# When next bits, totals and last values are issued in a hashed attention with a ReLU-squared feed-forward

## The chip, the cores and the metric

The kernel runs on one core of a Trainium2 chip. The metric is the device time of one launch in microseconds (us). In the profile the engines are PE (TensorE's matrix products) and PEld (its weight loads), DVE (VectorE), ACT (ScalarE), POOL (GpSimd) and SP (SyncE, which here only issues transfers). A line such as L419 is line 419 of the kernel before. A name with a q, such as POOLq, is the engine's sequencer.

## The reference, cut to what matters

```python
# q, k, v: (4, 8, 768, 64); proj: (64, 6); w_in: (512, 2048); w_out: (2048, 512)
q_bits = (einsum('bhsd,dk->bhsk', q, proj) > 0)
k_bits = (einsum('bhsd,dk->bhsk', k, proj) > 0)
mask = bucket(q_bits)[..., :, None] == bucket(k_bits)[..., None, :]   # all 6 bits agree
scores = where(mask, q @ k.T / sqrt(64), -1e9)
attn = softmax(scores)                       # rows divided by their sum + 1e-9
x = (attn @ v) as (3072 tokens, 512)         # heads side by side
h = x @ w_in
out = (max(h, 0) ** 2) @ w_out
```

Two queries and keys see each other only if their six hash bits agree. What comes out of the attention goes through a feed-forward layer with a squared ReLU.

## The kernel before, in words

The program is written in the order in which each engine shall issue (a manual schedule): engines run beside each other, each takes its own instructions in order, and waits between them follow from the data.

**Pairs.** The 32 heads are worked on as 16 pairs (`pr` from 0 to 15, `NP` is 16). In a pair the two heads lie in the two halves of the 128 partitions. Keys are cut into 6 blocks of 128 (`kt`), queries into two halves of 384 (`i`). `score(pr, kt, i)` makes one block of scores in PSUM: products of the bits (which push pairs of unequal bits far down) and products of the features, and then one ACT operation, exp, writes the result to `e`, a ring of four tiles (L459). Twelve such scores make a pair.

**Values.** `attend(pr, kt, s)` adds the products of `e` with the values to the accumulator `xo`, 64 rows of the array by 64 columns at a time; s says which half of the rows goes with which half of the queries. A pair's products lag behind its scores, so `attend(old, 4, 0)`, `attend(old, 5, 0)`, `attend(old, 4, 1)` and `attend(old, 5, 1)` of the pair before stand between the first scores of a pair. Whenever s changes, `part` (lines 499 to 504) puts a step between the last product before and the first product after: an empty instruction on POOL (L502) that waits for the one, and that the other waits for. In an even pair this comes at `attend(old, 4, 1)`, `attend(pr, 0, 1)` and `attend(pr, 2, 0)`; in an odd pair also in the sums of the totals.

**Totals.** `add_up` (L490, L495, DVE) adds the `e` of the six key blocks. In an odd pair, `sums_and_hashes` sums the totals of the two pairs before over the partitions by products with ones (`tot`, L564), and between them hashes the next two pairs (L382) and takes the signs (L401, ACT). `invert` (L600 to L608, DVE) makes the reciprocals, `spread` (L618, ACT) lays them out, `normalize` (L624, L630, DVE) multiplies the values kept by `keep_x` (L538, ACT), and one transfer on SP's queue writes them to `x_all` in DRAM.

**Bits of the next pair.** After the signs, `weigh` (L408, ACT) scales them, and `place_bits` (L419) sends eight transfers on POOL's queue that put them where the next pair's scores read them. There are two buffers of bits, for even and odd pairs. Before, both come in the middle of each pair: the weighing after `score(pr, 2, 1)`, the transfers after `attend(pr, 0, 1)`.

**Weights beside.** Between these steps each pair also rounds one piece of the 64-bit weights (`part_power`, `place_power`, `part_top`, `round_weight`), and from pair 4 on `sum_in` makes sums of weight blocks that the feed-forward part needs; 16 of them are dealt out over the pairs.

**After the attention.** The feed-forward part takes tokens in 3 chunks of 1024 and saves products by sums of blocks (a scheme of seven products for eight). `sum_x(0, n)` makes the four differences of x blocks for the first chunk, on DVE; `product` (L899) runs the seven products, with x and a unit of weights (`w_unit`) in the first two and a difference in the third. The first chunk's x was loaded during pairs 9 to 12. `keep_busy` at the very start makes products whose result nobody uses, while the first inputs are on their way.

Of the kernel before, what the change touches and what calls it, by code (L numbers as in the profile page):

```python
# [34 lines left out]
def kernel(  # L35
# [315 lines left out]
    busy = const.tile([P, P], BF16, name="busy")  # L351
    void = ps_o.tile([P, 2, 512], FP32, name="xo")

    def keep_busy(n):

        wide = busy.rearrange("p (o n) -> p o n", o=1).to_broadcast([P, 4, P])
        for _ in range(n):
            nc.tensor.matmul(
                out=void[:, 0].rearrange("p (o n) -> p o n", o=4), lhsT=busy, rhs=wide,
                start=True, stop=True,  # L360
            )

# [122 lines left out]
    def add_up(pr, kt):  # L485

        e = key_of(pr, kt)[:, :, :, 0:HS]
        if kt == 1:
            totals[pr] = to_add[(pr + 1) % 2]
            nc.vector.scalar_tensor_tensor(  # L490
                out=totals[pr], in0=key_of(pr, 0)[:, :, :, 0:HS], scalar=SB * TINY,
                in1=e, op0=ALU.add, op1=ALU.add,
            )
        else:
            nc.vector.tensor_tensor(out=totals[pr], in0=totals[pr], in1=e, op=ALU.add)  # L495
# [58 lines left out]
    def sum_up(pr, s, whole=False):  # L554

        to, n = tots[pr]
        halves = [(slice(0, P), s)] if whole else [
            (slice(r * HK, (r + 1) * HK), (r + s + n) % 2) for r in range(2)
        ]
        for rows, c2 in halves:  # L560
            for c in range(2):
                for h in range(2):
                    g = 2 * h + c
                    done = nc.tensor.matmul(  # L564
                        out=to[g * 32:(g + 1) * 32, c2], lhsT=ones[rows],
                        rhs=totals[pr][rows, h, c, c2 * QS:(c2 + 1) * QS],
                        start=whole or s == 0, stop=whole or s == 1, skip_group_check=True,
                    )
                    if s and not whole and "tot" in lasts:
                        part(lasts.pop("tot"), done)  # L570
        if not whole:
            lasts["tot"] = done

    def sum_whole(prs):

        new_totals(prs)
        for pr in prs:
            for s in range(2):
                sum_up(pr, s, True)

    def sums_and_hashes(prs, nexts):

        if not nexts:
            return sum_whole(prs)
        new_totals(prs)
        sum_up(prs[0], 0)
        for n, nxt in enumerate(nexts):
            hash_bits(nxt, turn("hash"))  # L590
            signs(nxt)
            if n < len(prs):
                sum_up(prs[n], 1)
            if n + 1 < len(prs):
                sum_up(prs[n + 1], 0)

    def invert(pr):

        flip = p_n.tile([P, HS], FP32, name="flip")
        nc.vector.transpose(  # L600
            out=flip.rearrange("p (c f) -> p c f", c=2), in_=spares.pop(pr)
        )
        once = p_n.tile([P, NB], FP32, name="once")
        nc.vector.reciprocal(
            out=once, in_=flip.rearrange("p (n f) -> p n f", f=32)[:, :, 0]
        )
        rec = p_n.tile([P, 2, NB], FP32, name="rec")
        nc.vector.tensor_copy(  # L608
            out=rec, in_=once.rearrange("p (o n) -> p o n", o=1).to_broadcast([P, 2, NB])
        )  # L610
        onces[pr] = once, rec
# [62 lines left out]
    todo = list(range(16))  # L674
    sums = {}
    for pr in range(NIN, NP):
        n = 1 + pr % 2
        sums[pr], todo = todo[:n], todo[n:]

    def load_x(i, fs=slice(0, NFT)):  # L680
# [27 lines left out]
    with tc.manual_schedule():  # L708
        nc.gpsimd.memset(busy, 1.0)
        nc.vector.memset(projs, 0.0)  # L710
        load_first()
        keep_busy(6)
        make_identity(nc, ident)
        constants()
        load_pair(1)
# [13 lines left out]
        for pr in range(NP):  # L729
            more, old, odd = pr + 1 < NP, pr - 1, pr % 2  # L730

            def beside(kt, s):
                if pr > 0:
                    attend(old, kt, s)

            if pr == 0:
                load_pair(2)
            elif pr + 3 < NP:
                load_pair(pr + 3)
            if 0 < pr < NP - 2:  # L740
                features(pr + (2 if pr > 1 else 1))
            if pr == 0:
                first_score()
                first_keys(1, spare("hash"))
            else:
                score(pr, 0, 0)
                attend(old, 4, 0)
                score(pr, 0, 1)
                attend(old, 5, 0)
                add_up(old, SB - 1)  # L750
                if not odd:
                    invert(pr - 2)
                if pr == 1:
                    features(3)
                    part_top(0)
                round_weight(old)
                if later:
                    later.pop(0)()
                if more:
                    load_weight(pr + 1)  # L760
                for m in sums.get(pr, ()):
                    sum_in(m)
            score(pr, 1, 0)
            beside(4, 1)
            score(pr, 1, 1)
            beside(5, 1)
            if pr == 0:
                features(1)
                load_pair(3)
            else:  # L770
                keep_x(old)
                if odd:
                    sums_and_hashes(
                        range(max(pr - 2, 0), pr), [n for n in (pr + 1, pr + 2) if n < NP]
                    )
            add_up(pr, 1)


            if pr in (X_0 + 1, X_0 + 2):
                load_unit(pr - X_0 - 1)  # L780
            part_power(pr)
            if odd and pr > 1:
                invert(pr - 2)
            if pr == 0:
                attend(pr, 0, 0)
            score(pr, 2, 0)
            if odd:
                attend(pr, 0, 0)
            elif pr == 0:
                attend(pr, 1, 0)  # L790
            score(pr, 2, 1)
            if pr > 0:
                if pr > 1:
                    spread(pr - 2)
                if not odd:
                    attend(pr, 0, 0)
                attend(pr, 1, 0)
                if more:
                    weigh(pr + 1)
                else:  # L800
                    place_power(pr, 0, 0)
            else:
                hash_bits(1, turn("hash"))
                signs(1)
                weigh(1)
            score(pr, 3, 0)
            if pr > 0:
                place_power(pr, 0, int(not more))
            attend(pr, 0, 1)
            if more:  # L810
                place_bits(pr + 1, PARTS if pr else PARTS[:3])
            score(pr, 3, 1)
            attend(pr, 1, 1)
            add_up(pr, 2)
            if pr > 1:
                normalize(pr - 2)
            if pr > 0:
                if more:
                    place_power(pr, 0, 1)
                else:  # L820
                    place_power(pr, 1, 0)
            if not more:
                invert(old)
            add_up(pr, 3)
            if more:
                load_values(pr + 1)


            score(pr, 4, 0)
            if more:  # L830
                place_power(pr, int(pr > 0), 0)
            else:
                place_power(pr, 1, 1)
            attend(pr, 2, 1)
            if not more:
                spread(old)
                normalize(old)
            score(pr, 4, 1)
            if more:
                place_power(pr, int(pr > 0), 1)  # L840
            attend(pr, 3, 1)
            if 0 < pr < NP - 1:
                part_top(pr)
            score(pr, 5, 0)
            if pr == 0:
                place_power(0, 1, 0)
            if more:
                attend(pr, 2, 0)
            if pr == 0:
                place_bits(1, PARTS[3:])  # L850
            if 2 * PB < pr <= 2 * PB + NFT:
                load_x(0, slice(pr - 2 * PB - 1, pr - 2 * PB))
            score(pr, 5, 1, spare("st") if not more else None)
            attend(pr, 3, 0)
            if pr == 0:
                place_power(0, 1, 1)
            add_up(pr, 4)
        pr = NP - 1
        attend(pr, 2, 0)
        attend_whole(pr, SB - 2)  # L860
        add_up(pr, SB - 1)
        sum_whole((pr,))
        invert(pr)
        for n in (1, 2, 3):
            sum_x(0, n)
        spread(pr)
        attend_whole(pr, SB - 1)
        keep_x(pr)
        normalize(pr)
        sum_x(0, 4)  # L870
        part_top(pr)
# [870 lines left out]
```

## Time and profile before

| | us |
|---|---|
| median of 3 runs | 861.4 (858.39 to 862.23) |
| profiled execution, own time | 860.77 |
| its span, first to last instruction | 859.2 |
| PE busy / DVE busy / ACT busy / POOL busy | 849.3 / 748.3 / 401.0 / 169.0 |
| mean granted TensorE clock | 0.997 |
| attention, up to the first feed-forward product | 321.3 |

The span is divided by place: the attention runs to 321.3 us, pair after pair, and the feed-forward part takes the rest. A timeline row has the start and the length in us, the engine, the line, the operation, what it writes and reads, and the count; a bracket at the end gives the idle time of the engine before it and what ended that.

### The profile page before, as it was taken

Reading aid. Unit: us, or ns where it says so; the run is one execution under the profiler, and the core shown is the slowest. Engines: PE = TensorE matmul, PEld = TensorE weight load, DVE = VectorE, ACT = ScalarE, POOL = GpSimd, SP = SyncE. Lnnn points to the kernel's source line nnn. Section 1 sums busy time; section 2 is a strip of 40 time slices with the busy share of each in tenths; the row PEclk is TensorE's granted clock in tenths of the full one; section 3 lists DMA queues with packets and bytes.
Section 4 is the critical chain, followed back from the end, with each engine's and each line's share of the span. In section 5 each row is a group of like instructions: output and inputs, shape, how many; then the busy total and the mean of one; then the engine's idle time right before and its main releaser. Section 6 shows DMA issues by size and latency. Waiting matters only on the chain.

```text
span 859.2 us, 17029 instructions
## 1 busy us (share of the span) xinstructions
PE 849.3 (99%) x6593; PEld 554.8 (65%) x6593; DVE 748.3 (87%) x1025; ACT 401.0 (47%) x752; POOL 169.0 (20%) x282
## 2 busy tenths in 40 slices
PE   8999999999999999999999999999999999999998
PEld 4555555555575544444688876667888766668886
DVE  5898999999999988988899978888988788889777
ACT  5887777778777752222111135554111255551111
POOL 1321111113231101653121221111000211100003
PEclk9999999999999999999999999999999999999999
DMA  9966998899996516999977995537647874335467
GB/s 214 169 122 146 179 187 192 190 186 230 273 219 205 168 63 221 326 282 288 352 244 241 265 216 180 176 123 250 221 148 185 184 241 164 133 114 166 141 172 146
DMA packets 234101, 170.13 MB, mean 198 GB/s; under 512 B 164712, under 2 KB 193200, under 8 KB 234016
## 3 DMA queue, kind: packets, MB, share of 16 engines
q1 hardware_dynamic: 194320, 87.78, 41.7%
q0 software_dynamic: 16512, 42.45, 16.0%
q10 hardware_dynamic: 23184, 38.78, 14.6%
q8 instruction: 53, 0.87, 0.4%
q14 instruction: 32, 0.26, 0.1%
HBM read 127.14 MB, written 41.16 MB: 196 GB/s over the span
## 4 chain that ended last, share of the span: by engine, by line
PE 84%; DVE 8%; ACT 3%; issue 2%; DMA 1%; POOL 0%; DVEq 0%; SPq 0%; ACTq 0%; POOLq 0%
PE acc L899 39%; PE acc L1163 13%; PE st L453 12%; PE xo L507 9%; PE acc L1116 8%; DVE t_x L495 2%; DVE total L495 1%; ACT e L459 1%; PE tot L564 1%; PE hash L382 1%; DMA out_dram<-h 1%; DMA bits<-signed 1%; DVE total L490 1%; DVE top L193 1%; DVE x_raw L630 0%
## 5 line engine op out<-in xcount | busy, mean ns | idle before, releaser
L459 ACT ACTIVATE e<-st 128x768 f32<-128x768 f32 x192 | 155.3, 810 | 60.4 <-PE st L453 57.8
L507 PE MATMUL xo<-e,v_nat 64*64 64x385 f32 (+1 forms) x1520 | 162.1, 485 | 0.0
L899 PE MATMUL acc<-b,leaf 128*128 128x256 f32 x600 | 133.0, 379 | 0.0
L899 PEld LDWEIGHTS acc<-b,leaf 128*128 128x128 f32 x600 | 113.9, 190 | 16.0 <-issue 0.5
L453 PE MATMUL st<-feat 64*64 64x384 f32 x1056 | 111.7, 483 | 0.1
L419 POOL DMA_DIRECT2D bits<-signed x120 | 62.8, 528 | 217.2 <-ACT signed L408 152.9
L507 PEld LDWEIGHTS xo<-e,v_nat 64*64 64x64 f32 (+1 forms) x1520 | 67.1, 133 | 57.8 <-issue 48.5
L1163 PE MATMUL acc<-t_x,w_unit 128*128 128x512 f32 x192 | 90.9, 595 | 0.0
L899 PE MATMUL acc<-t,leaf 128*128 128x256 f32 x336 | 75.9, 379 | 0.0
L453 PE MATMUL st<-bits 64*64 64x384 bf16 x768 | 70.4, 324 | 1.6 <-ACT e L459 1.0
L899 PEld LDWEIGHTS acc<-t,leaf 128*128 128x128 f32 x336 | 63.8, 190 | 8.7
L976 DVE SCALAR_TENSOR_TENSOR b<-h 128x512 f32<-128x512 f32 x96 | 65.7, 691 | 3.0
L495 DVE TENSOR_TENSOR total<-total,e 128x1536 f32<-128x1536 f32 x32 | 55.9, 1747 | 4.3 <-ACT e L459 3.9
L495 DVE TENSOR_TENSOR t_x<-t_x,e 128x1536 f32<-128x1536 f32 x32 | 55.8, 1745 | 2.9 <-ACT e L459 2.8
L453 PEld LDWEIGHTS st<-feat 64*64 64x64 f32 x1056 | 43.6, 133 | 20.5 <-issue 18.1
L899 PE MATMUL acc<-x,w_unit 128*128 128x512 f32 x128 | 56.5, 593 | 0.0
L453 PEld LDWEIGHTS <-bits 64*64 64x64 bf16 x768 | 29.8, 106 | 37.4 <-issue 34.6
L899 PE MATMUL acc<-b_t,leaf 128*128 128x256 f32 x240 | 53.8, 379 | 0.0
L906 ACT COPY two<-acc 128x256 f32<-128x256 f32 (+1 forms) x29 | 12.5, 431 | 87.5 <-PE acc L899 66.1
L1163 PEld LDWEIGHTS acc<-t_x,w_unit 128*128 128x128 f32 x192 | 35.8, 190 | 26.7 <-issue 23.0
L1284 POOL DMA_DIRECT2D out_dram<-h x24 | 15.6, 657 | 181.9 <-DVE h L1279 181.9
L453 PE MATMUL st<-t_x 64*64 64x384 f32 x480 | 50.6, 482 | 0.0
(189 smaller groups left out, 1371.0 us busy)
## 6 DMA issues: line engine op xcount, KB each, us to landing
leaf<-w_out ACTq DMA_DIRECT2D x142, 256.0 KB, 3.0
raw<-in_moe_w_in_dram SPq DMA_DIRECT2D x8, 1024.0 KB, 6.3
raw<-in_moe_w_out_dram SPq DMA_DIRECT2D x8, 1024.0 KB, 6.9
w_unit<-w_in SPq DMA_DIRECT2D x16, 512.0 KB, 4.0
w_unit<-w_in SPq DMA_DIRECT2D x8, 896.0 KB, 8.5
w_out<-sums POOLq DMA_DIRECT2D x16, 448.0 KB, 7.1
v_nat<-in_v_dram SPq DMA_DIRECT2D x16, 384.0 KB, 5.2
x_all<-x_raw SPq DMA_DIRECT2D x16, 384.0 KB, 3.2
```

Source lines behind the costliest of these rows:

```text
L193: nc.vector.scalar_tensor_tensor(out=one, in0=raw[:, :, :, 0], scalar=2.0**-32, in1=top, op0=ALU.mult, op1=ALU.add,)
L419: nc.gpsimd.dma_start(out=t[h * D:h * D + NBITS + 1, w, c * HS:(c + 1) * HS], in_=signed[pr % 2][at:at + NBITS + 1, h],)
L453: nc.tensor.matmul(out=st[k * HK:(k + 1) * HK, h, 0:HS], lhsT=src[1][rows, key], rhs=src[0][rows, cut], start=first, stop=not first, skip_ ...
L459: nc.scalar.activation(out=key_of(pr, kt)[:, :, i, 0:HS], in_=st[:, :, 0:HS], func=ACTF.Exp, scale=scale)
L495: nc.vector.tensor_tensor(out=totals[pr], in0=totals[pr], in1=e, op=ALU.add)
L507: return nc.tensor.matmul(out=outs[pr][h * D:(h + 1) * D, c, 0:HS + 1], lhsT=nat[pr, "v_nat"][rows, h, kt * D:(kt + 1) * D], rhs=key_of(pr ...
L899: nc.tensor.matmul(out=acc[to], lhsT=a(i), rhs=b(i), start=first and i == 0, stop=last and i == n - 1, skip_group_check=True,)
L906: nc.scalar.copy(out=t, in_=acc[of])
L976: nc.vector.scalar_tensor_tensor(out=out, in0=h, scalar=0.0, in1=h, op0=ALU.max, op1=ALU.mult)
L1116: nc.tensor.matmul(out=out, lhsT=w(a), rhs=b, start=start, stop=stop, skip_group_check=True)
L1163: nc.tensor.matmul(out=to, lhsT=w[:, PLACE[a], f], rhs=bt[b](f), start=first and f == 0, stop=last and f == NFT // 2 - 1, skip_group_check ...
L1284: queue.dma_start(out=out[at, m0 + a * 32:m0 + (a + 1) * 32].rearrange("(c i) j -> i c j", i=32), in_=ot[a * 32:(a + 1) * 32].rearrange("i ...
```

## The change

In words, part by part:

- *Even pairs:* weighing and the eight transfers of the bits of the next pair come right after `attend(old, 5, 0)`, ahead of `score(pr, 1, 0)` and `attend(old, 4, 1)`. In odd pairs they stay where they were.
- *Odd pairs:* `invert(pr - 2)` comes right behind the block of sums and hashes from pair 5 on, ahead of the addition of totals `add_up(pr, 1)`; `once` and `rec` have two buffers; `spread(pr - 2)` comes one step earlier in all pairs.
- *The last pair and the end:* `invert(old)` comes early and `normalize(old)` goes behind the last totals; the last value products `attend_whole(pr, SB - 1)` come ahead of the last totals `sum_whole((pr,))`; `keep_x(pr)` and `sum_x(0, 1)` come before `invert(pr)`.
- *Weights:* pairs 8 and 14 make no sum of weights, pair 15 makes two; `part_top` of odd pairs comes after their last addition.
- *Start:* after the six unused products comes one more of half the width.

```diff
-    def keep_busy(n):
+    def keep_busy(*ns):
...
+        for n in ns:
             nc.tensor.matmul(
-                out=void[:, 0].rearrange("p (o n) -> p o n", o=4), lhsT=busy, rhs=wide,
+                out=void[:, 0, 0:n * P].rearrange("p (o n) -> p o n", o=n), lhsT=busy,
+                rhs=busy.rearrange("p (o n) -> p o n", o=1).to_broadcast([P, n, P]),
...
         if not nexts:
+            keep_x(prs[-1])
             return sum_whole(prs)
         new_totals(prs)
-        sum_up(prs[0], 0)
-        for n, nxt in enumerate(nexts):
+        steps = [(pr, s) for pr in prs for s in range(2)]
+        if len(prs) > 1:
+            keep_x(prs[-1])
+            sum_up(*steps.pop(0))
+        for nxt in nexts:
             hash_bits(nxt, turn("hash"))
             signs(nxt)
-            if n < len(prs):
-                sum_up(prs[n], 1)
-            if n + 1 < len(prs):
-                sum_up(prs[n + 1], 0)
+            if len(prs) == 1 and nxt == nexts[0]:
+                keep_x(prs[0])
+            for _ in range(min(len(steps), len(prs))):
+                sum_up(*steps.pop(0))
...
-        n = 1 + pr % 2
+        n = 2 if pr % 2 else int(pr not in (NP // 2, NP - 2))
...
-        keep_busy(6)
+        keep_busy(4, 4, 4, 4, 4, 4, 2)
...
                 score(pr, 0, 1)
                 attend(old, 5, 0)
+                if not odd:
+                    weigh(pr + 1)
+                    place_bits(pr + 1)
                 add_up(old, SB - 1)
...
-                keep_x(old)
                 if odd:
                     sums_and_hashes(
                         range(max(pr - 2, 0), pr), [n for n in (pr + 1, pr + 2) if n < NP]
                     )
+                    if not more:
+                        part_power(pr)
+                    if pr > NIN:
+                        invert(pr - 2)
+                else:
+                    keep_x(old)
             add_up(pr, 1)
...
-            part_power(pr)
-            if odd and pr > 1:
+            if more:
+                part_power(pr)
+            else:
+                invert(old)
+            if odd and 1 < pr < NIN:
                 invert(pr - 2)
...
             score(pr, 2, 0)
+            if pr > 1:
+                spread(pr - 2)
...
-                if more:
+                if not more:
+                    place_power(pr, 0, 0)
+                elif odd:
                     weigh(pr + 1)
-                else:
-                    place_power(pr, 0, 0)
...
             attend(pr, 0, 1)
-            if more:
+            if more and (odd or pr == 0):
                 place_bits(pr + 1, PARTS if pr else PARTS[:3])
...
-            if not more:
-                invert(old)
             add_up(pr, 3)
...
                 spread(old)
-                normalize(old)
...
-            if 0 < pr < NP - 1:
+            if pr > 0 and more and not odd:
                 part_top(pr)
...
             add_up(pr, 4)
+            if odd and more:
+                part_top(pr)
         pr = NP - 1
         attend(pr, 2, 0)
         attend_whole(pr, SB - 2)
         add_up(pr, SB - 1)
+        attend_whole(pr, SB - 1)
         sum_whole((pr,))
+        keep_x(pr)
+        sum_x(0, 1)
         invert(pr)
-        for n in (1, 2, 3):
-            sum_x(0, n)
+        sum_x(0, 2)
+        sum_x(0, 3)
         spread(pr)
-        attend_whole(pr, SB - 1)
-        keep_x(pr)
+        normalize(old)
         normalize(pr)
         sum_x(0, 4)
```

More of the change, by code (lines that the diff above doesn't have):

```diff
@@ L352 @@
     void = ps_o.tile([P, 2, 512], FP32, name="xo")
-    def keep_busy(n):
-        wide = busy.rearrange("p (o n) -> p o n", o=1).to_broadcast([P, 4, P])
-        for _ in range(n):
+    def keep_busy(*ns):
+        for n in ns:
             nc.tensor.matmul(
-                out=void[:, 0].rearrange("p (o n) -> p o n", o=4), lhsT=busy, rhs=wide,
+                out=void[:, 0, 0:n * P].rearrange("p (o n) -> p o n", o=n), lhsT=busy,
+                rhs=busy.rearrange("p (o n) -> p o n", o=1).to_broadcast([P, n, P]),
                 start=True, stop=True,
@@ L602, in invert @@
         )
-        once = p_n.tile([P, NB], FP32, name="once")
+        once = p_n.tile([P, NB], FP32, name="once", bufs=2)
         nc.vector.reciprocal(
@@ L606, in invert @@
         )
-        rec = p_n.tile([P, 2, NB], FP32, name="rec")
+        rec = p_n.tile([P, 2, NB], FP32, name="rec", bufs=2)
         nc.vector.tensor_copy(
@@ L792 @@
             if pr > 0:
-                if pr > 1:
-                    spread(pr - 2)
                 if not odd:
```

## The prediction

> **What bounds the kernel now.** I read the page first, then the windows and the timelines of single pairs of heads in the attention, then the waits and the timelines around the place where the attention hands over to the feed-forward part.
>
> ```profile
> span 859.2 us, 17029 instructions
> PE 849.3 (99%) x6593; PEld 554.8 (65%) x6593; DVE 748.3 (87%) x1025; ACT 401.0 (47%) x752; POOL 169.0 (20%) x282
> ```
>
> TensorE (PE) is busy almost throughout. A busy share can hide slow work, so the next view is the windows, one row for each pair (pairs 3, 5, 7, 9, 10 and, from a second answer, pair 4 and three stretches around the hand-over). After the stretch come its length and then the busy time of PE, PEld, DVE, ACT, POOL; the third number from the right is the granted TensorE clock.
>
> ```profile
> core 0: us, PE busy (x) PEld busy (x) DVE busy (x) ACT busy (x) POOL busy (x), PEclk, DMA share, GB/s
> 66.15:86.63 20.48, 20.48 (x340) 10.98 (x336) 17.73 (x17) 15.68 (x24) 4.22 (x8) 1.00 0.65 136
> 104.08:124.98 20.90, 20.52 (x340) 10.98 (x336) 19.84 (x19) 15.67 (x24) 4.22 (x8) 1.00 1.08 194
> 142.43:163.35 20.92, 20.52 (x340) 10.98 (x336) 19.82 (x19) 15.67 (x25) 4.22 (x8) 1.00 0.88 193
> 180.80:201.57 20.77, 20.51 (x340) 10.98 (x336) 19.70 (x19) 15.67 (x24) 4.80 (x9) 1.00 1.04 218
> 201.57:219.63 18.06, 17.92 (x245) 10.01 (x241) 17.92 (x18) 13.98 (x22) 4.66 (x9) 1.00 0.96 234
> ...
> 86.60:104.05 17.45, 17.45 (x244) 9.82 (x240) 17.28 (x18) 14.03 (x22) 4.15 (x8) 1.00 0.81 184
> 314.39:317.81 3.42, 1.39 (x20) 0.48 (x20) 2.88 (x2) 0.00 (x0) 0.00 (x0) 1.00 0.32 115
> 317.81:321.22 3.41, 3.41 (x20) 0.92 (x12) 2.44 (x5) 0.79 (x4) 0.00 (x0) 0.50 0.00 0
> 321.22:324.63 3.41, 3.41 (x10) 1.63 (x9) 3.32 (x4) 1.39 (x2) 0.00 (x0) 1.00 0.00 0
> ```
>
> An even pair takes 17.45 us with PE busy for all of it; an odd one adds hashes and totals and takes 20.48. So within the pairs any time that PE loses is lost to the kernel, and no slack gives it back. Little is there to win: pairs 5, 7 and 9 are 0.42, 0.44 and 0.29 us longer than pair 3, and one place stands out, the hand-over, where PE is busy 1.39 of 3.42 us and then runs 3.41 us at half clock.
>
> **Even pairs send the next bits at once: the costly part.** Here weighing (L408, ACT) and the eight transfers of the bits (L419, POOL) of the next pair move ahead of `score(pr, 1, 0)` and `attend(old, 4, 1)`. What is moved past is POOL's queue. `attend(old, 4, 1)` is the first product of the old pair on the other half of its accumulator (s from 0 to 1), and at each such switch `part` puts an empty step on POOL (L502): it waits for PE's last product before the switch, and PE's next product waits for it. Before, that step came while POOL had nothing queued. Now eight transfers stand ahead of it in POOL's program, the first waits for the weighing on ACT, and PE, in order, waits behind all this with everything that follows.
>
> PE around this switch in pair 4, then ACT (the exp of the second score of pair 4; a weighing in pair 3 and what follows it), then POOL's transfers and its own steps in pair 3:
>
> ```profile
> 88.47 0.36 PE L453 MATMUL st<-bits 64*64 64x384 bf16 x4
> 88.64 0.84 PE L453 MATMUL st<-feat 64*64 64x384 f32 x8
> 89.28 0.84 PE L507 MATMUL xo<-e,v_nat 64*64 64x385 f32 x8
> ```
>
> ```profile
> 88.09 0.81 ACT L459 ACTIVATE e<-st 128x768 f32<-128x768 f32 x1 [0.64 <-PE st L453]
> ...
> 78.07 0.94 ACT L408 ACTIVATE signed<-signed,gains 128x768 bf16<-128x768 bf16 x1
> 78.91 0.79 ACT L459 ACTIVATE e<-st 128x768 f32<-128x768 f32 x1
> ```
>
> ```profile
> 79.29 4.23 POOL L419 DMA_DIRECT2D bits<-signed  x8 [16.83 <-PE st L453]
> ...
> L419 POOL DMA_DIRECT2D bits<-signed x8: 521/521/596, 79.3 to 82.9; - x8
> L419 POOLq EVENT_SEMAPHORE  x5: 17/17/17, 79.3 to 81.4; - x5
> ...
> L502 POOLq EVENT_SEMAPHORE  x1: 17/17/17, 82.9 to 82.9; - x1
> ...
> PEld xo L507 <- POOLq L502: 6.3, 40, 0.2
> ```
>
> The products of the switch are due at 89.28. The exp starts at 88.09 and takes 0.81; operations on ACT overlap by 0.10 (78.07 + 0.94 against 78.91), so the weighing would run from 88.80 to 89.74. POOL's first transfer begins 0.28 us after the weighing's end (79.01, 79.29): 90.02. How fast does POOL get past the eight? Its sequencer's five own waits between the transfers stand from 79.3 to 81.4, 0.52 us apart, one for each transfer: it does not run ahead, it hands over the next transfer when the last one is done. And the empty step of pair 3 came at 82.9, when the eighth started. So the eighth starts at 90.02 + 7 x 0.52 = 93.66 and the step passes at about 93.7: PE waits 4.4 us. The bounds: 0.7 us, if the step passes with the first transfer, and 5.2, if it passes only after all eight (4.23) and the weights are then loaded afresh (0.2). I take 4.4, by the step that the trace shows beside the eighth's start. It happens in pairs 2, 4, 6, 8, 10, 12 and 14: 7 x 4.4 = 30.8 us.
>
> A wait of 4.4 us also touches the clock. In the windows a stretch with 2.0 us of idle PE was followed by 3.41 us at 0.50, which costs half of it, 1.7 us. Each of the seven waits leaves a stretch of 3.4 us with at least 2.2 idle, more than that 2.0. Bounds: 0, and two such stretches, 3.4, where a wait lies across a boundary; I take one each: 7 x 1.7 = 11.9.
>
> [...]
>
> **The last pair and its totals.** The end of the attention on PE, ACT and DVE:
>
> ```profile
> PE tot L564 <- DVE total L495: 2.0, 1, 2.0
> ...
> 312.49 2.91 PE L507 MATMUL xo<-e,v_nat 64*64 64x385 f32 x24
> 317.43 1.20 PE L564 MATMUL tot<-total,ones 128*32 128x192 f32 x16 [2.03 <-DVE total L495]
> 318.56 2.81 PE L507 MATMUL xo<-e,v_nat 128*64 128x385 f32 x8
> 321.30 3.70 PE L899 MATMUL acc<-x,w_unit 128*128 128x512 f32 x8
> ...
> 311.74 2.22 ACT L459 ACTIVATE e<-st 128x768 f32<-128x768 f32 x3
> ...
> 311.82 0.97 DVE L624 STREAM_TRANSPOSE recs<-rec 128x768 f32<-128x768 f32 x1
> 312.82 1.02 DVE L630 SCALAR_TENSOR_TENSOR x_raw<-x_raw,recs 128x768 f32<-128x768 f32 x1
> 313.76 3.61 DVE L495 TENSOR_TENSOR total<-total,e 128x1536 f32<-128x1536 f32 x2
> 318.68 0.58 DVE L600 STREAM_TRANSPOSE flip<-tot 128x384 f32<-128x384 f32 x1 [1.30 <-PE tot L564]
> ...
> 319.64 1.22 DVE L647 TENSOR_TENSOR t_x<-x 128x1024 f32<-128x1024 f32 x1
> 320.89 1.23 DVE L647 TENSOR_TENSOR t_x<-x,t_x 128x1024 f32<-128x1024 f32 x1
> ```
>
> The totals' products wait 2.03 us for DVE's last addition, while the last eight value products (their e is done at 313.96) stand behind them. The change swaps the two, and moves the normalizing of pair 14 (0.97 + 1.02 us) behind the additions, which would then end at about 315.7, limited by that exp; the value products cover that time. The wait goes, and with it the half clock that followed: -2.0 - 1.7 = -3.7. What is late next is DVE: 2 us of normalizing and four differences come with the first feed-forward products. Those products, 3.70 us of them, read x and w_unit, which are in place; then PE wants the second difference, at 317.6 + 3.7 = 321.3. DVE would have the first by 316.9 (1.22), invert when the totals' products are through (from 317.6, 0.96 from the start of the transposing to the next operation) and have the second by about 319.8: 1.5 us in time, so I book nothing. Were that cover gone, the price is what the differences are late, up to the 2 us of normalizing.
>
> **Odd pairs invert behind the totals, and what pair 11 waits for.**
>
> ```profile
> 115.56 0.83 ACT L618 COPY rec<-once 32x12 f32<-32x12 f32 x4 [0.44 <-DVE rec L608]
> ...
> 212.21 5.95 DMA bits<-signed
> 218.29 1.29 PE st L453 x12
> ```
>
> In pairs 5, 7, 9 ACT stands 0.44 us for the inverse; taken ahead of an addition of 1.75 us it comes in time: -(0.42 + 0.44 + 0.29) = -1.2. Two buffers for `once` and `rec` only loosen it. Pair 11 waits for bits sent late in pair 10 (18.06 against 17.45): -0.6. The sums of weights merely move between pairs, to places where DVE is busy 17.3 of 17.45 us or less; 0, with 0.7 us each if not hidden. `part_top` likewise.
>
> **One more unused product.**
>
> ```profile
> 1.23 2.74 PE L358 MATMUL xo<-busy 128*128 128x512 bf16 x6 [1.23 <-POOL busy L709]
> 4.39 0.99 PE L338 MATMUL tp<-ident,qk_nat 128*64 128x128 f32 x6 [0.41 <-POOL bits L268]
> ```
>
> Half of one of these six is 0.2 us and lies in the gap of 0.41 before the transposes: 0. It may bring the clock up a stretch earlier (to -1.7) or delay the transposes (+0.2).
>
> **Sum.** The profiled execution took 860.8 (span 859.2 and 1.6 around it), 0.6 under the median of 861.4. 860.8 + 30.8 + 11.9 - 3.7 - 1.2 - 0.6 = 898.0.
>
> **Rivals.**
> (a) POOL's step is not held by the transfers, so the change is not slower. Its price is then only the weighing that POOL's first transfer waits for, 0.7 us: 7 x 0.7 = 4.9 against gains of 5.5, 860.2. It decides where the wait is below 0.8 us a pair. Against it stand the sequencer's waits, one each 0.52 us; for it, that no step in the trace was seen held: all were released by PE.
> [...]
> (b) The waits stand, but the clock does not fall: 898.0 - 11.9 = 886.1. Only one fall in the attention is on record, so this is not excluded.
> [...]
> (d) The early sending does nothing at the switch at all, and the gains stand alone: 860.8 - 5.5 = 855.3. The order of the code speaks against it: the transfers are placed before `attend(old, 4, 1)`, whose step is made there.
>
> **How the numbers follow.** My forecast has 0.70, (a) 0.07, (b) 0.10, (c) 0.08, (d) 0.05. The range reaches from (b), less a stretch of clock at the start, to the long waits: 885 to 908 (7 x 0.8 more for a wait of 5.2, and a second slow stretch in two or three pairs); it leaves out (a), (d) and the tails of the rest. A measurement can tell about 0.5% from no change, 4.3 us: (d) is faster, (a) the same, the others slower: 0.05, 0.07, 0.88.
>
> **What would show it.** PE waiting for POOL's step at the line of `part`, seven times about 4.4 us; even pairs of some 23.5 us; seven or more stretches at clock 0.50 between pairs 2 and 14; no wait of the last totals, and the feed-forward part starting without half clock. I am wrong if even pairs still take 17.5 us, or if the steps pass while POOL's transfers are still being issued.

## The result, and the profile after

The changed kernel takes 899.63 us (median of 6 runs, 898.32 to 900.55) where the kernel before takes 860.66 (median of 6, 858.02 to 862.23): ratio 1.0458, 95% interval 1.0437 to 1.0478. Its profiled execution took 900.17 us. First the head of its page, with the row of the clock in the page before and after, and PE's waits (total, times, longest). Line numbers are those of the kernel profiled: L419, L453, L502 and L507 are the same in all of them, and `product` is L915 here.

```profile
PEclk9999999999999999999999999999999999999999
```

```profile
span 898.6 us, 17030 instructions
PE 863.9 (96%) x6594; PEld 534.7 (60%) x6594; DVE 749.9 (83%) x1025; ACT 404.0 (45%) x752; POOL 167.5 (19%) x282
...
PEclk9989898989998989999999999999999999999999
```

```profile
PE xo L507 <- POOLq L502: 28.5, 7, 4.1
PE xo L357 <- POOL busy L713: 1.2, 1, 1.2
PE acc L1331 <- DVE o L1281: 0.5, 1, 0.5
```

A wait that did not exist before leads: seven times about 4.1 us for the empty step on POOL. The row of the clock, full before (the first of the two), dips all through the attention. The wait of the last totals is gone from the list. The timelines of PE, ACT and POOL show one of the seven, in pair 4, and two rows give the moments of the first and the last transfer and of the step (nanoseconds of one, then the first and the last start).

```profile
94.88 0.81 PE L453 MATMUL st<-feat 64*64 64x384 f32 x8
99.78 1.56 PE L507 MATMUL xo<-e,v_nat 64*64 64x385 f32 x8 [4.08 <-POOLq L502]
...
94.32 0.81 ACT L459 ACTIVATE e<-st 128x768 f32<-128x768 f32 x1 [0.64 <-PE st L453]
95.03 0.93 ACT L408 ACTIVATE signed<-signed,gains 128x768 bf16<-128x768 bf16 x1
...
96.24 4.14 POOL L419 DMA_DIRECT2D bits<-signed  x8 [6.71 <-ACT signed L408]
...
L419 POOL DMA_DIRECT2D bits<-signed x8: 518/518/521, 96.2 to 99.9; - x8
...
L502 POOLq EVENT_SEMAPHORE  x2: 17/17/17, 89.2 to 99.7; - x2
```

The weighing ends at 95.96, the first transfer starts at 96.24, and the step passes at 99.7, just before the eighth's start at 99.9; PE goes on at 99.78. Now windows: pairs 2, 4 and 10 (even) and 3 and 11 (odd), then the windows of the clock around the wait in pair 4.

```profile
core 0: us, PE busy (x) PEld busy (x) DVE busy (x) ACT busy (x) POOL busy (x), PEclk, DMA share, GB/s
47.93:72.54 24.61, 20.53 (x244) 9.14 (x240) 17.96 (x17) 14.31 (x22) 4.13 (x8) 0.86 0.42 97
72.54:92.87 20.33, 20.33 (x340) 10.03 (x336) 17.39 (x16) 15.66 (x25) 4.13 (x8) 1.00 0.61 130
92.87:117.20 24.33, 20.25 (x244) 9.09 (x240) 18.86 (x19) 14.31 (x22) 4.13 (x8) 0.86 0.70 145
226.49:249.90 23.41, 19.36 (x244) 9.26 (x240) 18.47 (x18) 14.31 (x22) 4.65 (x9) 0.93 0.84 196
249.90:270.24 20.34, 20.34 (x340) 10.05 (x336) 18.91 (x19) 15.87 (x25) 4.64 (x9) 1.00 0.92 232
...
94.79:98.20 3.41, 0.91 (x16) 0.22 (x8) 3.34 (x6) 1.87 (x3) 1.95 (x4) 1.00 1.17 156
98.20:101.61 3.41, 1.83 (x16) 0.92 (x20) 2.30 (x3) 0.00 (x0) 2.18 (x5) 0.50 0.88 226
101.61:105.02 3.41, 3.41 (x32) 1.30 (x28) 1.17 (x1) 1.54 (x2) 0.00 (x0) 0.50 0.79 280
105.02:108.44 3.42, 3.42 (x52) 1.64 (x48) 1.53 (x3) 2.49 (x7) 0.00 (x0) 1.00 0.03 5
```

Pair 4 is 24.33 us long, 17.45 before. In it PE worked at the same products for 20.25 us instead of 17.45: the rest of the loss is the clock, at 0.50 through two whole windows, not one. Pair 10, 23.41 us, has one. Odd pairs run at full clock and are a little shorter than before. The end of the attention on PE:

```profile
355.83 4.21 PE L507 MATMUL xo<-e,v_nat 64*64 64x385 f32 x32
359.97 0.86 PE L564 MATMUL tot<-total,ones 128*32 128x192 f32 x16
360.76 1.55 PE L915 MATMUL acc<-x,w_unit 128*128 128x512 f32 x3
```

Values, totals and feed-forward products follow one another without a gap. From the first exp of pair 15 to the first feed-forward product it is 21.6 us, 25.5 before, and the feed-forward part from there takes as long as before, 537.9 us.

### The profile page after: what moved, and what is told of

The parts are those of the page before. It is cut to its first block, busy times and chain, and to the rows that moved or that the text cites. A ratio compares the mean times of both kernels' runs of the same rounds, so it can differ in the third digit from the quotient of the medians.

```text
span 898.6 us, 17030 instructions
## 1 busy us (share of the span) xinstructions
PE 863.9 (96%) x6594; PEld 534.7 (60%) x6594; DVE 749.9 (83%) x1025; ACT 404.0 (45%) x752; POOL 167.5 (19%) x282
## 4 chain that ended last, share of the span: by engine, by line
PE 88%; issue 6%; POOL 3%; DMA 1%; DVE 0%; ACT 0%; POOLq 0%; ACTq 0%; DVEq 0%
PE acc L915 39%; PE st L453 14%; PE acc L1179 12%; PE xo L507 12%; PE acc L1132 8%; POOL bits L419 3%; PE tot L564 1%; DMA bits<-signed 1%; PE hash L382 1%; PE tp L338 0%; PE xo L357 0%; DMA out_dram<-h 0%; DVE bits L433 0%; DVE tmp L1281 0%; ACT e L459 0%
## 5 line engine op out<-in xcount | busy, mean ns | idle before, releaser
L507 PE MATMUL xo<-e,v_nat 64*64 64x385 f32 (+1 forms) x1520 | 164.6, 509 | 28.5 <-POOLq L502 28.5
L915 PE MATMUL acc<-b,leaf 128*128 128x256 f32 x600 | 133.0, 379 | 0.0
L915 PEld LDWEIGHTS acc<-b,leaf 128*128 128x128 f32 x600 | 113.9, 190 | 16.0 <-issue 0.5
L507 PEld LDWEIGHTS xo<-e,v_nat 64*64 64x64 f32 (+1 forms) x1520 | 57.0, 138 | 101.7 <-issue 61.6
L453 PE MATMUL st<-feat 64*64 64x384 f32 x1056 | 111.9, 498 | 0.1
L419 POOL DMA_DIRECT2D bits<-signed x120 | 62.0, 520 | 225.5 <-ACT signed L408 207.8
L915 PE MATMUL acc<-t,leaf 128*128 128x256 f32 x336 | 75.9, 379 | 0.0
L915 PEld LDWEIGHTS acc<-t,leaf 128*128 128x128 f32 x336 | 63.8, 190 | 8.7
L453 PE MATMUL st<-bits 64*64 64x384 bf16 x768 | 67.4, 338 | 0.3 <-DVE bits L437 0.2
L453 PEld LDWEIGHTS st<-feat 64*64 64x64 f32 x1056 | 39.8, 138 | 29.6 <-issue 26.5
L915 PE MATMUL acc<-x,w_unit 128*128 128x512 f32 x128 | 56.5, 593 | 0.0
L915 PE MATMUL acc<-b_t,leaf 128*128 128x256 f32 x240 | 53.8, 379 | 0.0
L453 PE MATMUL st<-t_x 64*64 64x384 f32 x480 | 52.0, 509 | 0.0
L915 PEld LDWEIGHTS acc<-b_t,leaf 128*128 128x128 f32 x240 | 45.6, 190 | 6.2
```

The lines of the kernel that those rows point to most:

```text
L419: nc.gpsimd.dma_start(out=t[h * D:h * D + NBITS + 1, w, c * HS:(c + 1) * HS], in_=signed[pr % 2][at:at + NBITS + 1, h],)
L453: nc.tensor.matmul(out=st[k * HK:(k + 1) * HK, h, 0:HS], lhsT=src[1][rows, key], rhs=src[0][rows, cut], start=first, stop=not first, skip_ ...
L507: return nc.tensor.matmul(out=outs[pr][h * D:(h + 1) * D, c, 0:HS + 1], lhsT=nat[pr, "v_nat"][rows, h, kt * D:(kt + 1) * D], rhs=key_of(pr ...
L915: nc.tensor.matmul(out=acc[to], lhsT=a(i), rhs=b(i), start=first and i == 0, stop=last and i == n - 1, skip_group_check=True,)
```

## The experiments

Medians and ratios are against runs of the kernel before on the same chip in the same turn.

### Transfers late again

```diff
                 if not odd:
                     weigh(pr + 1)
-                    place_bits(pr + 1)
...
-            if more and (odd or pr == 0):
+            if more:
                 place_bits(pr + 1, PARTS if pr else PARTS[:3])
```

> The kernel after, with one thing undone: the eight transfers of an even pair come again behind attend(pr, 0, 1); the weighing stays early. Theory (the switch step on POOL is held behind the transfers, and the waits pull the clock down): no wait of PE for L502, even pairs of 17.5 us, clock 1.00 from the first raise to the end, and what is left are the gains of the other edits, 39.4 - 47.1 = -7.7 against the pairs of before at best: 852 to 855 us. Rival (the early weighing on ACT, or moved DVE work, makes even pairs long): it stays above 880.

Measured: 854.69 us, ratio 0.9941 (0.9923 to 0.9959). The seven waits are gone, and the clock holds. The rows are pair 4, then pair 12 and the one wait for bits:

```profile
85.11:102.56 17.45, 17.45 (x244) 8.27 (x240) 17.28 (x18) 13.93 (x22) 4.56 (x8) 1.00 0.93 189
236.42:255.56 19.14, 17.88 (x245) 14.13 (x241) 19.00 (x18) 14.16 (x22) 4.97 (x9) 1.00 0.91 216
...
PE st L453 <- DMA bits<-signed: 1.3, 1, 1.3
```

Pair 12 is long, since PE waits 1.3 us at its end for the bits of pair 13, which are again sent late. Apart from that, the early weighing and the other edits cost nothing; the place of the eight transfers carries the loss, and without it the change is a gain.

### Half of the transfers early

```diff
                 if not odd:
                     weigh(pr + 1)
-                    place_bits(pr + 1)
+                    place_bits(pr + 1, PARTS[:2])
...
-            if more and (odd or pr == 0):
-                place_bits(pr + 1, PARTS if pr else PARTS[:3])
+            if more:
+                place_bits(pr + 1, (PARTS if odd else PARTS[2:]) if pr else PARTS[:3])
```

> The kernel after, but in even pairs only four of the eight transfers go early, the other four behind attend(pr, 0, 1). Theory: the step passes as the fourth starts, so each wait is 4.07 - 4 x 0.52 = 2.0 us, 7 x 2.0 = 14 above e1_late_bits; the clock falls in some of the seven stretches (2.0 us of idle did it once at the hand-over before), 0 to 1.7 each: 868 to 880 us. Rival (the wait is for the weighing, or for the landing of the transfers, and not for their hand-over one by one): waits stay at 4 us and the time at 895 or more, or fall to 0.7 us and 860 or less.

Measured: 877.21 us, ratio 1.0202 (1.0176 to 1.0229). PE's waits, the transfers of pair 4 and the step behind them:

```profile
PE xo L507 <- POOLq L502: 15.1, 7, 2.2
...
91.76 2.08 POOL L419 DMA_DIRECT2D bits<-signed  x4 [6.71 <-ACT signed L408]
...
L502 POOLq EVENT_SEMAPHORE  x1: 17/17/17, 93.3 to 93.3; - x1
```

(`PARTS` has four parts of two transfers each.) The step passes as the fourth transfer starts (91.76 + 3 x 0.52 = 93.3). Four transfers fewer take 1.9 us off each wait, 0.48 each: the wait is for POOL to hand them over one by one, neither for the weighing alone nor for their landing. With a wait of 2.2 us the clock fell in only two of the seven pairs of the profiled execution, for one window each. That execution took 873.62 us with a mean clock of 0.995; the other three took 877.1 to 877.4 at 0.991, so more of their waits cost a window. Here is a window that kept the clock, in pair 2, and one that halved it, in pair 8, each with the window after it:

```profile
51.20:54.61 3.41, 1.41 (x20) 0.79 (x24) 3.29 (x6) 0.80 (x2) 2.07 (x4) 1.00 0.04 6
54.61:58.03 3.42, 3.42 (x52) 1.72 (x48) 2.59 (x3) 3.02 (x7) 0.00 (x0) 1.00 0.77 283
170.66:174.08 3.42, 1.26 (x20) 0.41 (x16) 3.35 (x5) 1.85 (x3) 1.97 (x4) 1.00 1.40 194
174.08:177.49 3.41, 3.41 (x28) 1.49 (x24) 1.28 (x3) 0.81 (x1) 0.10 (x1) 0.50 0.89 265
```

### Transfers right behind the step

```diff
                 if not odd:
                     weigh(pr + 1)
-                    place_bits(pr + 1)
...
             beside(4, 1)
+            if pr > 0 and not odd:
+                place_bits(pr + 1)
             score(pr, 1, 1)
```

> The kernel after, but the eight transfers of an even pair come right behind attend(old, 4, 1), one score later, so that the switch step stands ahead of them in POOL's program. Theory: the step of that switch is not held, and the next one comes 5.8 us later, when the eighth has started 0.8 us before: no waits, as e1_late_bits, 852 to 855 us. Rival (sending early collides with other transfers or with DVE wherever it stands): even pairs longer than 18 us, over 860.

Measured: 854.03 us, ratio 0.9928 (0.9900 to 0.9956): faster than both kernels; it does not differ by what can be told from the kernel with late transfers. POOL and pair 4:

```profile
89.56 4.14 POOL L419 DMA_DIRECT2D bits<-signed  x8 [6.71 <-ACT signed L408]
...
86.19:103.64 17.45, 17.45 (x244) 8.28 (x240) 17.28 (x18) 13.93 (x22) 4.13 (x8) 1.00 0.92 189
```

The eight go 3.37 us after the pair's first exp (86.19), just as in the changed kernel (96.24 - 92.87), since the weighing sets their start. All seven even pairs take 17.45 us, and PE does not wait for bits as it did in pair 12 of the run with late transfers. Sending at once cost nothing; that the step stood behind them in POOL's program cost everything.

### The wait filled with unused products

```diff
             score(pr, 1, 0)
+            if pr > 0 and not odd:
+                junk = turn("junk")
+                for _ in range(19):
+                    nc.tensor.matmul(
+                        out=junk[:, 0, 0:4 * P].rearrange("p (o n) -> p o n", o=4), lhsT=busy,
+                        rhs=busy.rearrange("p (o n) -> p o n", o=1).to_broadcast([P, 4, P]),
+                        start=True, stop=True,
+                    )
             beside(4, 1)
```

> The kernel after with 19 unused products of 512 columns (19 x 0.216 = 4.1 us of work, into a PSUM buffer that nobody reads) ahead of attend(old, 4, 1) of every even pair, so that PE works where it waited. Theory: the wait is only filled, the clock stays at 1.00, and even pairs take 17.45 + 4.1 to 4.3: the 18.6 us that even pairs lose beyond the waits go away, 880 to 883 us. Rival (what even pairs lose beyond the wait is catching up on ACT or DVE, or the products merely add): 899 or more.

Measured: 883.67 us, ratio 1.0273 (1.0245 to 1.0301), 16.0 us less than the changed kernel's 899.63 (measured in another turn) and just above the range that was expected.

```profile
92.76 4.28 PE L774 MATMUL junk<-busy 128*128 128x512 bf16 x19
...
90.00:111.81 21.81, 21.81 (x263) 10.47 (x259) 18.86 (x19) 14.15 (x23) 4.13 (x8) 1.00 0.85 164
```

Pair 4 takes 17.45 + 4.36 us. The 19 products took 4.28 us, 0.225 each. With PE busy the clock stayed at 1.00, and what even pairs lost beyond the wait is gone: it was the clock.

### One part at a time, on the kernel before

```diff
                 attend(old, 5, 0)
+                if not odd:
+                    weigh(pr + 1)
+                    place_bits(pr + 1)
                 add_up(old, SB - 1)
...
-                if more:
+                if not more:
+                    place_power(pr, 0, 0)
+                elif odd:
                     weigh(pr + 1)
-                else:
-                    place_power(pr, 0, 0)
...
-            if more:
+            if more and (odd or pr == 0):
                 place_bits(pr + 1, PARTS if pr else PARTS[:3])
```

> The kernel before with one part of the change alone: in even pairs the weighing and the eight transfers come early. Theory: it carries the whole loss, 7 x (4.07 + 2.66) = 47.1 us less the 0.6 that pair 11 no longer waits: 906 to 909 us. Rival (part of the loss comes from how it meets the other edits): under 900.

Measured: 903.6 us, ratio 1.0507 (1.0486 to 1.0528), +43.4 us. The early weighing and transfers alone carry more than the whole loss. That is below the 906 to 909 that were expected: in the profiled execution two pairs had only one slow window, and the odd pairs came down to 20.47 us by themselves. ACT no longer waits for the inverse in them; that DVE caught up during the waits would explain it, but no run shows it apart.

```diff
-                normalize(old)
...
         add_up(pr, SB - 1)
+        attend_whole(pr, SB - 1)
         sum_whole((pr,))
+        keep_x(pr)
         invert(pr)
         for n in (1, 2, 3):
             sum_x(0, n)
         spread(pr)
-        attend_whole(pr, SB - 1)
-        keep_x(pr)
+        normalize(old)
         normalize(pr)
```

> The kernel before with the end of the attention alone changed: last values ahead of the last totals, normalize(old) behind them, with two buffers of once and rec, which that order needs. Theory (the wait of 2.03 us and half of the 3.41 us at clock 0.50 go): -3.7 us, about 856.7. Rival (the clock falls there whatever the order, or DVE's differences come late for the first feed-forward products): -2.0 or less, 858.4 or more.

(`once` and `rec` have two buffers here as well.) Measured: 858.49 us, ratio 0.9991 (0.9976 to 1.0005), -1.7 us: by its time this is the rival's case (858.4 or more), and it is not to be told from no change. The profile shows the full gain at its place (21.6 us from the first exp of pair 15 to the first feed-forward product, where the kernel before has 25.5), but also a wait for bits, in pair 4:

```profile
PE st L453 <- DMA bits<-signed: 1.0, 1, 1.0
```

And nearly half of the gain is the clock, which is a matter of chance: of the 29 executions of the kernel before in this turn, 16 have a mean granted clock of 0.999 or 1.000, which leaves no room for a whole window at half clock (1.7 of 859 us is 0.002). In the median, then, little more than the 2.0 us of the wait could be won, and the interval does not exclude that.

```diff
+                    if pr > NIN:
+                        invert(pr - 2)
...
-            if odd and pr > 1:
+            if odd and 1 < pr < NIN:
                 invert(pr - 2)
...
             score(pr, 2, 0)
+            if pr > 1:
+                spread(pr - 2)
...
             if pr > 0:
-                if pr > 1:
-                    spread(pr - 2)
```

> The kernel before with the odd pairs' part alone: invert(pr - 2) right behind the block from pair 5 on, spread one step earlier, two buffers of once and rec. Theory (ACT no longer waits for the inverse in pairs 5, 7 and 9): -1.2 us by the prediction, -2.2 if each of the six odd pairs comes to the 20.33 us that they have in the kernel after. Rival (the wait only moves to the addition that is now behind the inversion): 0.

(Here too `once` and `rec` have two buffers.) Measured: 857.86 us, ratio 0.9974 (0.9961 to 0.9987), -2.4 us: the larger of the two figures. Pair 5 is 20.32 us with PE busy throughout. The hand-over is written as in the kernel before and has much the same wait (2.20 us, 2.03 before), and yet its clock does not fall:

```profile
315.46 0.86 PE L564 MATMUL tot<-total,ones 128*32 128x192 f32 x16 [2.20 <-DVE total L495]
...
310.85:314.27 3.42, 2.40 (x20) 0.63 (x12) 3.31 (x3) 0.56 (x1) 0.00 (x0) 1.00 0.32 115
314.27:317.68 3.41, 2.22 (x24) 0.90 (x24) 2.36 (x5) 0.20 (x1) 0.00 (x0) 1.00 0.00 0
```

A window's boundary falls into the wait: 1.02 us is idle in the one window and 1.19 in the other, and the clock stayed at 1.00.

```diff
         keep_busy(6)
+        keep_busy(1, 2)
```

> The kernel before with the one more unused product of half width alone. Theory: it lies in the 0.41 us before the first transposes, 0 us; the clock's first rise moves between executions by itself. Rival (it brings the rise a stretch of 3.41 us earlier): up to -1.7 us.

(`keep_busy` here takes a second number, the width in blocks of 128.) Measured: 859.6 us, ratio 0.9993 (0.9979 to 1.0006): no difference that can be told. The records of the granted clock begin, at 1.00, at 7.19 us in the profiled execution before and at 6.04 in the changed kernel's. The boundaries of the clock's windows lay elsewhere even between profiled executions of kernels that begin alike: at 53.82 in the changed kernel, at 54.61 with half of the transfers early.

## Why the prediction was right

The forecast was 898.0 us, the median 899.63. The mechanism is the one named: the step was held behind the transfers (PE waited 4.1 us for it), against (a) and (d), and the clock fell to 0.50, against (b). No run speaks for (c), to which 0.08 was given: the seven windows of 3.41 us behind which the clock fell in the even pairs held 0.35 to 1.36 us of work. By its steps, against the profiled executions (39.4 us between their spans):

- *The waits.* Forecast 7 x 4.4 = 30.8. In pair 4 PE went on 4.26 us later than the 95.52 at which its products were due (94.88 + 0.64, as 88.64 to 89.28 before), so some 29.8. The step passed at 99.7, ahead of the eighth's start at 99.9 and with the seventh transfer still under way. Taken by the letter that meets a sign of being wrong, and it corrects the reading that POOL hands over a transfer only when the last one is done: it ran ahead by a part of one transfer, the step passing some 0.2 us before the eighth's start. It is also why the wait was a little shorter than forecast.
- *The clock.* Forecast 7 x 1.7 = 11.9, mis-sized: even pairs took 169.3 us together against 7 x 17.45 = 122.15, and 47.1 - 29.8 = 17.3 are the clock's. The bound was right and the value taken was too low. In six of seven pairs the clock was slow for two windows: the first still held the rest of the wait and was not full (1.40 to 2.40 us of work in 3.41), and only behind the second, which was full, did the clock come back. The first ones held 10.8 us of work together and lost half of it, 5.4; the seven full ones lost 7 x 1.7 = 11.9. Pair 10, with one slow window, lost 23.41 - 17.45 - 4.26 = 1.7, as forecast.
- *The end.* Forecast -3.7, profile -3.9. But the half clock in that sum belongs to the profiled execution, and not to every one; with the edit alone the median moved by 1.7 us. That the profile came out so close was chance in this part.
- *Odd pairs.* Forecast -1.2, alone -2.4. I counted pairs 5, 7 and 9 down to pair 3's 20.48, but pair 3 too became shorter, where only `spread` moves: the odd pairs come to 20.33, and pair 15 up to the end of its last exp from 18.1 to 17.7 (which the 3.9 of the end contain).
- *Pair 11.* -0.6, seen: pair 10 no longer ends in a wait for bits.
- *The unused product.* 0, as forecast. The first exp of pair 0 came 0.6 us earlier in the profiled execution; with the product alone the time did not move.
- *Two buffers* "only loosen" was wrong in its reason: with one buffer of `once` and `rec` the order at the end cannot be had, since the inverses of pairs 14 and 15 are then alive together. It changed no number.

The misses have opposite signs and partly cancel: 5.4 us too little for the clock, 1.0 too much for the waits, 2.2 more gained elsewhere. The mechanism was right; that the sum came within 1.6 us of the median was in part luck.

## What to carry to other kernels

When work moves ahead on a queue, look for what else that queue does: here an empty step that only orders two products of another engine held that engine for 4.1 us behind eight transfers and for 2.2 behind four. Put such a step ahead of the transfers: in the kernel at 854.03 us, which does so, the same early sending cost nothing. Price a new wait of a busy TensorE with its clock as well: here a wait of 4.1 us cost 6 to 7.

## What the runs showed of the hardware

In these runs POOL's sequencer did not get past its queue of transfers: it handed over one each 0.52 us, and an instruction with nothing to do waited its turn behind them. The empty step passed 3.5 us after the first of eight had started (96.24, 99.7) and 1.5 after the first of four (91.76, 93.3).

In the traces before and after, the changes of TensorE's granted clock lie whole windows of 3.41 us apart: from 98.20 to 234.73 in the changed kernel it is 136.53 us, 40 windows of 3.413. The length of a gap alone did not settle whether it fell: it did behind the hand-over's wait of 2.03 us in the kernel before, and did not behind the one of 2.20 us with the odd pairs' part alone. A window of the changed kernel in pair 10 with 1.42 us of work, and the one above with 1.41, kept the next at full clock; the next one of pair 10, with 1.36, and one with 1.39 before, halved it.

```profile
227.90:231.32 3.42, 1.42 (x20) 0.40 (x12) 3.35 (x6) 2.33 (x3) 1.45 (x3) 1.00 0.86 108
231.32:234.73 3.41, 1.36 (x20) 0.79 (x24) 2.40 (x3) 0.00 (x0) 2.64 (x6) 1.00 0.85 168
234.73:238.14 3.41, 3.41 (x29) 1.46 (x24) 1.99 (x2) 1.61 (x2) 0.00 (x0) 0.50 1.01 262
```

The edge was not sharp to hundredths. At the end of the kernel with the transfers behind the step, one with 1.43 us was followed by half clock:

```profile
846.63:850.05 3.42, 1.43 (x7) 0.74 (x5) 1.35 (x4) 0.27 (x1) 0.00 (x0) 1.00 0.59 103
850.05:852.00 1.95, 0.00 (x0) 0.00 (x0) 0.00 (x0) 0.00 (x0) 0.00 (x0) 0.50 0.19 52
```

So in these windows falls came with about 2.0 us of idle and more in one of them (1.43 us of work and less), some 60% of it. Coming back needed more work than that: slow windows with 1.83 us (98.20 in pair 4) and even 2.40 us (in pair 2) were followed by another slow one, and behind the seven waits only full ones raised the clock. What lies between was not seen there.

```profile
53.82:57.24 3.42, 2.40 (x20) 1.09 (x24) 0.88 (x1) 0.00 (x0) 1.63 (x4) 0.50 0.68 222
57.24:60.65 3.41, 3.41 (x28) 1.28 (x24) 1.73 (x2) 1.61 (x2) 0.00 (x0) 0.50 0.24 93
```

A wait of 2.0 to 2.2 us thus cost nothing more (2.20) or 1.7 us more (2.03), by where the windows' boundaries lay in that execution.
